# Query weights folded in three bursts instead of four, and the last tile of the hidden transform in slices of 384 and 128 columns

## The chip, the cores and the metric

One core of a Trainium2 chip. The metric is the device time of one launch, in microseconds; smaller is better. The core's engines run their own instruction streams: TensorE (PE; PEld is its weight load), VectorE (DVE), ScalarE (ACT), GpSimd (POOL) and SyncE (SP), which here only issues DMAs. PE accumulates into eight PSUM banks of 128 x 512 f32 (2 KB a partition). A float32 number is carried as a pair, high part and low part, and a product of two such matrices takes three matmuls.

## The reference

```python
def reference(A_x, A_dft_seq_re, A_dft_seq_im, A_dft_hid_re, A_dft_hid_im, B_x, B_w_q, B_k1, B_k2, B_u, B_v, gate_w):
    def _A_ref(x, dft_seq_re, dft_seq_im, dft_hid_re, dft_hid_im):
        a = jnp.einsum("bsd,ed->bse", x, dft_hid_re)
        b = jnp.einsum("bsd,ed->bse", x, dft_hid_im)
        y = jnp.einsum("ts,bse->bte", dft_seq_re, a) - jnp.einsum("ts,bse->bte", dft_seq_im, b)
        return y
    def _B_ref(x, w_q, k1, k2, u, v):
        q = jnp.einsum("nd,dhc->nhc", xf, w_q)
        s1 = jnp.einsum("nhd,ed->nhe", q[..., :dk], k1)
        s2 = jnp.einsum("nhd,ed->nhe", q[..., dk:], k2)
...
        act = _gelu(jnp.einsum("nd,nhkd->nhk", xf, ue))
        out = jnp.einsum("nhk,nhk,nhkd->nd", g, act, ve)
        return out.reshape(B, S, D)

    g = _sigmoid((x * gate_w).sum(-1, keepdims=True))
    a = _A_ref(x, A_dft_seq_re, A_dft_seq_im, A_dft_hid_re, A_dft_hid_im)
    b = _B_ref(x, B_w_q, B_k1, B_k2, B_u, B_v)
    return g * a + (1 - g) * b
```

Here x is 2048 x 640 (S x D), w_q is 640 x 32 x 256, k1 and k2 are 16 x 128, u and v 256 x 640. Branch A is a two-sided Fourier transform; branch B picks, for each token and head, the best two of 256 experts by the scores s1 and s2; g mixes the two.

## The kernel before

**Sequence transform.** The transform along the sequence runs first, in 128 *pieces*: two matrices (re, im), four chunks of 512 columns (TC) and, for each of them, 16 row tiles of x (NT). One piece multiplies five 128-column slices of an x tile (index d) with one 128 x 512 tile of the matrix: 5 x 3 = 15 matmuls, written by `mm3` (L140, L141, L142), accumulated in PSUM banks 0 to 4. After the 16th piece of a chunk ACT copies the five banks to the buffer ST (L248, called through `stage`), and the next piece, the first of the next chunk, opens the banks anew. DVE later multiplies ST by a row of gate values (L213, operand `grow`) and it goes to DRAM. A tile of the matrix is loaded (`wf`, L173) five pieces ahead, and split three pieces ahead: ACT takes its high part (L135), POOL or DVE subtracts it (L136). A tile of x is loaded as `xr`, split by `split_x` (ACT L135, DVE L136, into `X`), and summed against the gate's weights by `gate_sum` (DVE L314, into `zc`); behind piece 14 `gate` turns `zc` into g (ACT: table load and sigmoid, L541), and behind piece 15 `store_gate` writes it to DRAM in four small stores issued by ACT (L547, `gdr`). Split x tiles 0 to 11 are put away to DRAM one by one (`put_x`, L496, tile `xd`) so that their places are free, and come back later.

**Folding the query weights.** In the first 30 pieces (N0) the kernel also computes W' = w_q x keys, so that the scores need only x W' afterwards. W' has eight *groups* of four heads. A group has four w_q tiles of 640 KB (numbers 4G to 4G + 3, 32 tiles in all), and `w_part(m)` multiplies one of them: four matmuls of 32 x 320 (L405). Two tiles make a half group in bank 5, the next two in bank 6; behind each half DVE transposes it to SBUF (L411, `wp`), so a bank is free for the next group when that transpose is done. `split_w(G)` splits the group's result (ACT L135 and DVE L136, into `WU`); for groups 4 to 7 `make_t` and `split_t` also form sums of blocks. The tiles are multiplied in four *bursts* of two groups, behind pieces 10, 16, 22 and 27. A w_q tile is loaded on SP (L396) into a pool of five buffers, or into a place that is lent by something which is not in use just then: `LENT_WQ` names places of x tiles (X0 to X15) or of others, `LENT_U` two halves of the buffer `wqu`. The load waits until the last reader of that place is through.

**What sets the order.** `at(n, f)` hangs f behind piece n, and `follow(n)` calls what hangs there; each engine carries out its instructions in the order of these calls. So a load, a split or a sum that is hung one piece later stands later in the stream of SP, ACT or DVE, behind all that was hung before it. SP's and ACT's DMAs share eight slots, handed out in turn: an issue waits until the DMA that had the slot before has landed.

**The end.** After the pieces come the scores, the choice of experts, and 84 steps of the hidden transform. The last step's tile is 2 x 128 rows of d; its second half is held back and computed in two slices of columns of the same 512, each with 18 matmuls (six high and low pairs, three matmuls each), so that the first slice can be subtracted (DVE L1224) and stored (L1225, from SP, ACT, SP) while PE computes the second. The slices are 256 columns each (`c = TC // 2`).

Of the kernel before, what the change touches and what calls it, by code (L numbers as in the profile page):

```python
# [17 lines left out]
P = 128  # L18
S = 2048
D = 640  # L20
# [5 lines left out]
NT = S // P  # L26
NP = NT // 2
TC = 512
# [4 lines left out]
NG = HH // 8  # L33
# [73 lines left out]
def gated_mix_kernel(ctx: ExitStack, tc: tile.TileContext, xT, xn, dreT, dimT, wsre, wsim, wq, kT, uT, vv, gw, out):  # L107
# [14 lines left out]
    def bank(n, shape=(P, TC), dt=F32):  # L122
        return psum.tile(list(shape), dt, name=f"b{n}", tag=f"b{n}")
# [4 lines left out]
    ST = big.tile([P, 5, TC], F32, name="ST", tag="ST")  # L128
# [9 lines left out]
    def mm3(o, wh, wl, ah, al, first, last, more=False):  # L138

        nc.tensor.matmul(o, wh, ah, start=first, stop=False, skip_group_check=more)  # L140
        nc.tensor.matmul(o, wh, al, start=False, stop=False, skip_group_check=more)  # L141
        nc.tensor.matmul(o, wl, ah, start=False, stop=last, skip_group_check=more)  # L142
# [9 lines left out]
    def run_bg(us):  # L152
        bg.run(us, share)
# [38 lines left out]
    def at(n, f, *args):  # L192
        then.setdefault(n, []).append(lambda: f(*args))
# [57 lines left out]
    for q in range(2 * NC):  # L251
        n = NT * (q + 1)
# [84 lines left out]
    for n in range(WARM):  # L337
        c = slice(0, 2 * P) if n < WARM - 1 else slice(2 * P, TC)
# [41 lines left out]
    wqs, wps, wp = {}, {}, {}  # L380
    WQB = 5
    NWQ = 4 * NG
    BURST = 8
    LENT_WQ = {5: "X15", 6: "X14", 15: "xl", 16: "xf", 17: "xh", 23: "xl", 29: "X6", 30: "X7", 31: "X8"}
    LENT_U = {7: 1, 8: 0, 14: 1, 18: 0}

    def load_wq(m):


        if m in LENT_U:  # L390
            wqs[m] = wqu[:, LENT_U[m]]
        elif m in LENT_WQ:
            wqs[m] = big.tile([P, 4, HALF], F32, name="wq", tag=LENT_WQ[m])
        else:
            wqs[m] = p1.tile([P, 4, HALF], F32, name="wq", tag="wq", bufs=WQB)
        nc.sync.dma_start(wqs[m], wq[m // 4 * 4 + m % 2 * 2 + m // 2 % 2])  # L396
# [61 lines left out]
    xf, xs = {}, {}  # L458
# [40 lines left out]
        X[s] = place(tag)  # L499
        nc.sync.dma_start(X[s].bitcast(F32), xd[s])  # L500

    for s, b in enumerate((12, 14, 16, 17, 18, 19, 20, 21, 22)):
        at(b, put_x, s)
    for s, tag in ((11, "xh"), (12, "xl")):
        at(s + 12, move_x, s, tag)
    for n in range(NT - 4):
        at(n, load_x, n + 4)
    for n in range(NT - 3):
        at(n, split_x, n + 3)
    for n in range(NT - 2):  # L510
        at(n, gate_sum, n + 2)


    n = N0 - 1
    for B, b in enumerate((10, 16, 22, 27)):
        for m in range(BURST * B, BURST * (B + 1)):
            at(b, w_part, m)
        for G in (2 * B, 2 * B + 1):
            at(b, split_w, G)
            if G >= NG // 2:  # L520
                at(b + G % 2 * (G < NG - 1), make_t, G)
                at(b + 1 + G % 2 * (G < NG - 1), split_t, G)
    for b, m in enumerate((0, 1, 2, 3, 4, 5, 6, 7, 8)):
        at(b, load_wq, m)
    for m, b in enumerate((10, 10, 11, 11, 12, 13, 13, 15, 16, 16, 16, 17, 18, 19, 20, 20, 22, 22, 22, 22, 23, 24, 25), 9):
        at(b, load_wq, m)
    for s in range(9, AWAY):
        at(n - 3, put_x, s)
# [277 lines left out]
    for p in range(NP):  # L806
        n = N0 + 4 * p + min((p + 1) // 2, 3)
# [3 lines left out]
    for n in range(2 * NT + 3, 4 * NT + 3):  # L811
        s = n % NT
# [151 lines left out]
    def t_sum(k, n, a):  # L964

        m = 8 if k == KD else k
        if n < 2:
            return TS[m][:, (2 * n + a) * 2 * P:][:, :2 * P]
        if n == 2:
            return TS[5 + k // 2][:, (2 * (k % 2) + a) * 2 * P:][:, :2 * P]  # L970
        return right(0, a, k)[:, 2 * P:4 * P] if n == 3 else TS[m][:, PAIR + a * P:][:, :P]

    def right(w, a, k):
        return T[("xh", "xl")[a]][:, w] if k == KD else DD[k][:, w, a]
# [107 lines left out]
    for k, (n, m) in enumerate(((-1, 2), (0, 4), (5, 7), (7, 9), (10, 12))):  # L1082
        n, m = NT * (NC + 2) + n, NT * (NC + 2) + m
# [8 lines left out]
    def split_step(m):  # L1092
        if m < 2 * NSTEP:
            b, (u, k) = m // NSTEP, divmod(m % NSTEP, KZ)
            what = UNITS[u]
            key = (b, "s" if (b or k == KD) and what in ("s1", "s2", "s4") else what, k)
            sp[m] = ring(m)[:, 0], ring(m)[:, 1]
            split(raw[key], *sp[m], nc.vector if what in ("s2", "s3") else nc.gpsimd)
            bg.credit -= 0.8 if what in ("s2", "s3") else 0.0
            if what in ("a22", "s3", "s4") or k < KD and (b == 0 or what in ("a11", "a12")):  # L1100
                give(key)
# [30 lines left out]
    roles, res = {}, {"c22": ST[:, 0:2], "c": ST[:, 2:4]}  # L1132

    def put(b, row, d, f):
        c = slice((2 * b + row) * TC, (2 * b + row + 1) * TC)
        if d == 4:
            nc.scalar.dma_start(out[4][:, c], f)
        else:
            nc.scalar.dma_start(out[d:d + 2, :, c].rearrange("d p t -> p d t"), f)
# [33 lines left out]
    def step(m):  # L1173
        b, (u, k) = m // NSTEP, divmod(m % NSTEP, KZ)
        what = UNITS[u]
        if k == 0:
            if what in ("a11", "s1"):
                roles["W"] = bank(0)
            if what in ("a12", "a22"):
                roles["Z"] = [bank(2), bank(6)]  # L1180
            if what == "s1":
                roles["Y"] = [bank(3), bank(4)]
            if what == "a11":
                roles["X"] = [bank(5), bank(1)]
        split_step(m + AHEAD)
        o, w, w5 = {
            "a11": ("X", lambda a: right(0, a, k)[:, 0:2 * P], lambda a: right(0, a, k)[:, 4 * P:]),
            "a12": ("Z", lambda a: right(1, a, k)[:, 0:2 * P], lambda a: right(1, a, k)[:, 4 * P:]),
            "s1": ("Y", lambda a: t_sum(k, 0, a), lambda a: right(0, a, k)[:, 4 * P:]),
            "s2": ("X", lambda a: t_sum(k, 1, a), None),  # L1190
            "s4": ("Y", lambda a: right(1, a, k)[:, 2 * P:4 * P], None),
            "s3": ("X", lambda a: t_sum(k, 3, a), None),
            "a22": ("Z", lambda a: t_sum(k, 2, a), lambda a: t_sum(k, 4, a))}[what]
        h, l = sp.pop(m)
        more = what in ("s2", "s3", "s4")
        end = k == KD
        very_last = b == 1 and what == "a22"
        for d in range(1 if very_last else 2):
            c = slice(d * P, (d + 1) * P)
            mm3(roles[o][d], w(0)[:, c], w(1)[:, c], h, l, k == 0 and what in ("a11", "a12", "s1", "a22"), end, more)  # L1200
            run_bg(0.68)
        if very_last:
            held.append((t_sum(k, 2, 0)[:, P:], t_sum(k, 2, 1)[:, P:], h, l))
        if w5:
            mm3(roles["W"], w5(0), w5(1), h, l, k == 0 and what in ("a11", "s1"),
                end and what in ("a12", "a22"))
            run_bg(0.68)
        if not end:
            return
        if what in ("a12", "a22"):  # L1210
            f = ST[:, 4]
            nc.scalar.activation(f, roles["W"], AF.Copy)
            put(b, u // 6, 4, f)
        if what == "s3":
            at(NPC + m, post, b, what)
        elif not very_last:
            at(NPC + m + 1, post, b, what)
        else:
            z, c = (*roles["Z"], bank(7)), TC // 2
            for n, (d, r, eng) in enumerate(((0, slice(0, TC), nc.sync), (1, slice(0, c), nc.scalar), (1, slice(c, TC), nc.sync))):  # L1220
                if n:
                    for i, (wh, wl, h, l) in enumerate(held):
                        mm3(z[n][:, r], wh, wl, h[:, r], l[:, r], i == 0, i == KD)
                nc.vector.tensor_tensor(res["c"][:, d, r], res["c"][:, d, r], z[n][:, r], op=OP.subtract)  # L1224
                eng.dma_start(out[d][:, 3 * TC + r.start:3 * TC + r.stop], res["c"][:, d, r])  # L1225
# [61 lines left out]
    for m in range(2 * NSTEP):  # L1287
        share = 0.95 if m >= 5 else 0.0
        step(m)
        follow(NPC + m)  # L1290
        if m == NSTEP:
            bg.drain()
# [44 lines left out]
```

## Time and profile before

| | |
|---|---|
| median of 3 runs | 748.27 us (748.08 to 748.84) |
| the profiled execution, whole | 748.37 us |
| its span in the profile | 746.6 us |
| granted TensorE clock in the span | 1.0 |
| PE busy | 742.6 us |
| w_q loads into the pool and lent x places | 28 of 640 KB, 8.4 us from issue to landing |
| x tiles moved to DRAM | 11 of 640 KB, 9.7 us |
| sequence matrix tiles, first matrix | 63 of 256 KB, 6.8 us |

In the rows of the profile that follow, a row with a time is one instruction (start, duration, engine, line, operation, operands, shapes); what stands in brackets is how long its engine was idle before it and what ended that. A row without a time groups the instructions of a line: count, busy time and mean ns of one behind the bar, then the idle time ahead of them with its releaser. PE's instructions overlap, so their pace is read from their starts. `PEq`, `ACTq` and `SPq` rows are DMA issues.

### The profile page before, as it was taken

The page shows a single profiled execution, that of the slowest core. Times are in us where ns is not written, and L with a number is a line of the kernel's source. Part 1 is how long each engine was busy: PE and PEld are TensorE (multiplying, and loading weights), DVE is VectorE, ACT ScalarE, POOL GpSimd, SP SyncE. Part 2 cuts the span into 40 slices and gives each one's busy share as a digit, 9 for nine tenths or more (in the row PEclk, how much of TensorE's full clock was granted, in tenths as well). Part 3 has the DMA queues.
Part 4 walks back from the last instruction along what each step waited for, and adds up shares of the span by engine and source line. Part 5 has one row for each costly group of instructions (what it writes and reads, how often), then busy time and mean ns, then how long its engine had stood idle before and what let it go on. Part 6 is the DMA issues. An engine that isn't in the chain of part 4 may idle for free.

```text
span 746.6 us, 11142 instructions
## 1 busy us (share of the span) xinstructions
PE 742.6 (99%) x3923; PEld 604.7 (81%) x3923; DVE 579.7 (78%) x744; ACT 366.4 (49%) x664; POOL 343.4 (46%) x287
## 2 busy tenths in 40 slices
PE   9999999999999999999999999999999999999998
PEld 7877777888888888888888888888888888888887
DVE  7982277595999899999999888979799974367651
ACT  4434154553445745555453686633545643443351
POOL 5632424441532424245135456644455693487253
PEclk9999999999999999999999999999999999999999
DMA  9989999777656785971498676488856689775301
GB/s 336 403 310 373 413 375 380 217 226 221 155 158 151 192 246 136 254 201 63 124 403 279 151 172 193 138 258 283 286 200 197 228 265 334 224 234 175 113 29 71
DMA packets 84632, 171.11 MB, mean 229 GB/s; under 512 B 16096, under 2 KB 21600, under 8 KB 84320
## 3 DMA queue, kind: packets, MB, share of 16 engines
q1 hardware_dynamic: 71680, 147.44, 58.5%
q0 software_dynamic: 5472, 9.96, 8.5%
q10 hardware_dynamic: 7424, 13.00, 4.6%
q8 instruction: 31, 0.51, 0.3%
q14 instruction: 25, 0.20, 0.1%
HBM read 136.40 MB, written 32.39 MB: 226 GB/s over the span
## 4 chain that ended last, share of the span: by engine, by line
PE 99%; DVE 0%; issue 0%
PE b L140 31%; PE b L141 31%; PE b L142 31%; PE b L405 2%; PE b L240 2%; PE b L890 1%; PE b L339 0%; PE b L343 0%; DVE ST L1224 0%
## 5 line engine op out<-in xcount | busy, mean ns | idle before, releaser
L140 PE MATMUL b<-WS,X 128*128 128x512 f32 x620 | 242.9, 392 | 0.0
L141 PE MATMUL b<-WS,X 128*128 128x512 f32 x620 | 241.3, 389 | 0.0
L142 PE MATMUL b<-WS,X 128*128 128x512 f32 x620 | 241.3, 389 | 0.0
L136 POOL TENSOR_TENSOR WS<-wf,WS 128x512 fp32r<-128x512 f32 x89 | 133.5, 1502 | 163.9 <-ACT WS L135 157.0
L140 PEld LDWEIGHTS b<-WS,X 128*128 128x128 f32 x620 | 116.4, 188 | 26.3 <-issue 2.1
L142 PEld LDWEIGHTS b<-WS,X 128*128 128x128 f32 x620 | 116.4, 188 | 24.3
L141 PEld LDWEIGHTS b<-WS,X 128*128 128x128 f32 x620 | 116.4, 188 | 23.7
L135 ACT ACTIVATE WS<-wf 128x512 fp32r<-128x512 f32 x89 | 55.7, 627 | 82.8 <-PE b L142 51.9
L136 POOL TENSOR_TENSOR xl<-xf,xh 128x640 fp32r<-128x640 f32 x16 | 27.3, 1709 | 74.2 <-ACT xh L135 74.2
L878 DVE TENSOR_TENSOR hot<-rows,wtab 128x1024 f16<-128x1024 f16 x64 | 55.8, 897 | 5.6 <-PE b L890 5.6
L600 ACT ACTIVATE sc<-b 128x512 f32<-128x512 f32 x32 | 19.9, 621 | 78.8 <-PE b L142 75.0
L187 POOL DMA_DIRECT2D WS<-in_wsre x30 | 26.5, 882 | 61.8 <-ACT WS L185 60.5
L136 POOL TENSOR_TENSOR WS<-ra,WS 128x512 fp32r<-128x512 f32 x33 | 47.2, 1439 | 14.5 <-ACT WS L135 14.3
L848 ACT ACTIVATE b<-b,mask 128x128 f32<-128x128 f32 x128 | 43.1, 343 | 15.6 <-PE b L890 12.5
L135 ACT ACTIVATE WS<-ra 128x512 fp32r<-128x512 f32 x47 | 29.5, 631 | 43.0 <-PE b L142 25.7
L655 DVE TENSOR_TENSOR eq<-sc,mm 128x1024 f16<-128x1024 f32 x32 | 44.4, 1388 | 0.9
L662 DVE TENSOR_REDUCE tied<-eq 128x64 f32<-128x1024 f16 x32 | 39.0, 1219 | 0.9
L653 DVE TENSOR_REDUCE mm<-sc 128x64 f32<-128x1024 f32 x32 | 38.8, 1211 | 0.2
L213 DVE SCALAR_TENSOR_TENSOR ST<-ST,grow 128x512 f32<-128x512 f32 x40 | 29.7, 807 | 9.2 <-DMA grow<-gdr 9.2
L136 POOL TENSOR_TENSOR WP<-ra,WP 128x512 fp32r<-128x512 f32 x13 | 19.3, 1492 | 31.0 <-ACT WP L135 30.9
L140 PE MATMUL b<-WU,xh 128*128 128x512 f32 x80 | 31.2, 391 | 0.0
L142 PE MATMUL b<-WU,xl 128*128 128x512 f32 x80 | 31.1, 389 | 0.0
(218 smaller groups left out, 1447.4 us busy)
## 6 DMA issues: line engine op xcount, KB each, us to landing
X<-xd SPq DMA_DIRECT2D x36, 640.0 KB, 6.5
wq<-in_wq SPq DMA_DIRECT2D x28, 640.0 KB, 8.4
wf<-in_wsim SPq DMA_DIRECT2D x64, 256.0 KB, 4.7
wf<-in_wsre SPq DMA_DIRECT2D x63, 256.0 KB, 6.8
ra<-pd SPq DMA_DIRECT2D x40, 256.0 KB, 3.4
WS<-in_wsre POOLq DMA_DIRECT2D x30, 256.0 KB, 6.4
pd<-ST ACTq DMA_DIRECT2D x30, 256.0 KB, 4.8
xd<-X SPq DMA_DIRECT2D x11, 640.0 KB, 9.7
```

What stands on the lines that cost most here:

```text
L135: nc.scalar.activation(h, f, AF.Copy)
L136: eng.tensor_sub(l, f, h.bitcast(F32))
L140: nc.tensor.matmul(o, wh, ah, start=first, stop=False, skip_group_check=more)
L141: nc.tensor.matmul(o, wh, al, start=False, stop=False, skip_group_check=more)
L142: nc.tensor.matmul(o, wl, ah, start=False, stop=last, skip_group_check=more)
L187: nc.gpsimd.dma_start(l, (wsre, wsim)[w][c, s], accum_op=OP.add)
L213: nc.vector.scalar_tensor_tensor(f, f, -1.0 if w else 1.0, g, op0=OP.mult, op1=OP.mult)
L653: nc.vector.tensor_reduce(m, sc, op=OP.max, axis=AX.X)
L655: nc.vector.tensor_tensor(eq, sc, m[:, :, None].to_broadcast([P, HH, E]), op=OP.is_equal)
L662: nc.vector.tensor_reduce(tied[:, s, ib, :], eq, op=OP.add, axis=AX.X)
L848: nc.scalar.activation(f[:, :, n], f[:, :, n], AF.Copy, scale=mask4[:, n:n + 1])
L878: nc.vector.tensor_tensor(o, a, b, op=op)
```

## The change

The eight groups are folded in three bursts of 3, 3 and 2 groups, behind pieces 14, 21 and 27. The w_q tiles wait longer, so more of them need a lent place: tiles 8 and 9 lie in two halves of ST, tile 0 in the place of x tile 15, tiles 22 and 23 in those of x tiles 0 and 1. For this `split_x` and `gate_sum` of x tile 15 are called inside the first burst, behind group 0, while `split_w` of a burst's first group is called ahead of its third. The places of some `put_x` calls and of the w_q loads move with it. At the end, the two slices are 384 and 128 columns instead of 256 and 256.

```diff
-    BURST = 8
-    LENT_WQ = {5: "X15", 6: "X14", 15: "xl", 16: "xf", 17: "xh", 23: "xl", 29: "X6", 30: "X7", 31: "X8"}
-    LENT_U = {7: 1, 8: 0, 14: 1, 18: 0}
+    LENT_WQ = {0: "X15", 10: "xl", 11: "xf", 19: "xl", 20: "xf", 21: "xh", 22: "X0", 23: "X1", 29: "X6", 30: "X7", 31: "X8"}
+    LENT_U = {6: 1, 7: 0, 17: 1, 18: 0}
+    LENT_ST = {8: 0, 9: 1}
...
+        elif m in LENT_ST:
+            f = ST.rearrange("p a b -> p (a b)")[:, LENT_ST[m] * 2 * D:][:, :2 * D]
+            wqs[m] = f.rearrange("p (j c) -> p j c", j=4)
...
-    for s, b in enumerate((12, 14, 16, 17, 18, 19, 20, 21, 22)):
+    for s, b in enumerate((11, 12, 13, 16, 17, 18, 20, 21, 22)):
         at(b, put_x, s)
...
+    for n in range(NT - 4):
+        at(n, split_x, n + 3)
     for n in range(NT - 3):
-        at(n, split_x, n + 3)
-    for n in range(NT - 2):
         at(n, gate_sum, n + 2)
...
-    for B, b in enumerate((10, 16, 22, 27)):
-        for m in range(BURST * B, BURST * (B + 1)):
-            at(b, w_part, m)
-        for G in (2 * B, 2 * B + 1):
+    for b, G0, G1 in ((14, 0, 3), (21, 3, 6), (27, 6, 8)):
+        for G in range(G0, G1):
+            if G == G0 + 2:
+                at(b, split_w, G0)
+            for m in range(4 * G, 4 * G + 4):
+                at(b, w_part, m)
+            if G == 0:
+                at(b, split_x, NT - 1)
+                at(b, gate_sum, NT - 1)
+        for G in range(G0 + (G1 == G0 + 3), G1):
+            late = G == 5
             at(b, split_w, G)
             if G >= NG // 2:
-                at(b + G % 2 * (G < NG - 1), make_t, G)
-                at(b + 1 + G % 2 * (G < NG - 1), split_t, G)
-    for b, m in enumerate((0, 1, 2, 3, 4, 5, 6, 7, 8)):
-        at(b, load_wq, m)
-    for m, b in enumerate((10, 10, 11, 11, 12, 13, 13, 15, 16, 16, 16, 17, 18, 19, 20, 20, 22, 22, 22, 22, 23, 24, 25), 9):
+                at(b + late, make_t, G)
+                at(b + late + 1, split_t, G)
+    for m in range(10):
+        at(m, load_wq, m)
+    for m, b in enumerate((10, 12, 14, 14, 15, 15, 16, 16, 17, 17, 18, 18, 19, 20, 21, 21, 21, 22, 22, 23, 24, 25), 10):
         at(b, load_wq, m)
...
-            z, c = (*roles["Z"], bank(7)), TC // 2
+            z, c = (*roles["Z"], bank(7)), 3 * P
```

How it moves instructions is seen in the streams of three engines. In the rows that follow, `b_480` is a bank's tile, a `waits` list names the events that an issue waits for, and `xN` counts equal instructions in a row. The changed kernel's lines lie 3 to 10 further down (L411 is L414, L541 is L551, L547 is L557, L396 is L399, L496 is L499).

**DVE at the first burst.** First before (behind piece 10), from the last x tile ahead of it to the next one:

```order
L136 TENSOR_TENSOR X<-xr,X 128x640
L314 ISA xr,zc<-xr,gwb 128x640
L314 ISA zc 128x1
L411 STREAM_TRANSPOSE wp<-b_480 128x2x5x32
L411 STREAM_TRANSPOSE wp<-b_491 128x2x5x32
L411 STREAM_TRANSPOSE wp<-b_501 128x2x5x32
L411 STREAM_TRANSPOSE wp<-b_512 128x2x5x32
L136 TENSOR_TENSOR WU<-wp,WU 128x5x128 x2
L136 TENSOR_TENSOR X<-xr,X 128x640
```

and after (behind piece 14):

```order
L414 STREAM_TRANSPOSE wp<-b_569 128x2x5x32
L414 STREAM_TRANSPOSE wp<-b_580 128x2x5x32
L136 TENSOR_TENSOR X<-xr,X 128x640
L314 ISA xr,zc<-xr,gwb 128x640
L314 ISA zc 128x1
L414 STREAM_TRANSPOSE wp<-b_594 128x2x5x32
L414 STREAM_TRANSPOSE wp<-b_605 128x2x5x32
L136 TENSOR_TENSOR WU<-wp,WU 128x5x128
L414 STREAM_TRANSPOSE wp<-b_617 128x2x5x32
L414 STREAM_TRANSPOSE wp<-b_628 128x2x5x32
L136 TENSOR_TENSOR WU<-wp,WU 128x5x128 x2
```

The subtraction and the gate sum of x tile 15 now stand between the transposes of group 0 and those of group 1, and the subtraction of group 0's W' ahead of group 2's transposes.

**ACT between piece 12 and piece 16.** First before, up to the copies of the five banks and the gate's stores:

```order
L135 ACTIVATE X<-xr 128x640
L135 ACTIVATE WS<-wf 128x512 x2
L541 ACT_TABLE_LOAD
L541 ACTIVATE gt<-zc 128x16
L135 ACTIVATE WS<-wf 128x512
L248 ACTIVATE ST<-b_129 128x512
L248 ACTIVATE ST<-b_130 128x512
L248 ACTIVATE ST<-b_131 128x512
L248 ACTIVATE ST<-b_132 128x512
L248 ACTIVATE ST<-b_133 128x512
L547 DMA gdr<-gc 32x32 x4
```

and after:

```order
L135 ACTIVATE X<-xr 128x640
L135 ACTIVATE WU<-wp 128x5x128 x3
L551 ACT_TABLE_LOAD
L551 ACTIVATE gt<-zc 128x16
L135 ACTIVATE WS<-wf 128x512
L248 ACTIVATE ST<-b_129 128x512
L248 ACTIVATE ST<-b_130 128x512
L248 ACTIVATE ST<-b_131 128x512
L248 ACTIVATE ST<-b_132 128x512
L248 ACTIVATE ST<-b_133 128x512
L557 DMA gdr<-gc 32x32 x4
```

The three copies of W' of the first burst now stand just ahead of the gate's table load; before, its two copies stood behind piece 10, four pieces earlier.

**SP at the loads for the second burst**, with the events waited for. Before (the gate's stores have slots DMAHW4, 6, 0 and 1 in between):

```order
L396 DMA wq_731<-in_wq 128x1280 [waits DMAHW2_49,DVE_49]
L396 DMA wqu_87<-in_wq 128x1280 [waits DMAHW3_49,PE_49]
L396 DMA wq_734<-in_wq 128x1280 [waits DMAHW4_49,PE_49]
L173 DMA wf_736<-in_wsre 128x512 [waits DMAHW5_49,Pool_49]
L496 DMA xd_85<-X_193 128x1280 [waits DMAHW6_49]
L396 DMA wq_756<-in_wq 128x1280 [waits DMAHW7_49,PE_49]
```

and after (the gate's stores have slots DMAHW2, 4, 5 and 6 in between):

```order
L499 DMA xd_85<-X_193 128x1280 [waits DMAHW1_49]
L399 DMA wq_706<-in_wq 128x1280 [waits DMAHW2_49,PE_49]
L399 DMA wqu_87<-in_wq 128x1280 [waits DMAHW3_49,PE_49]
L173 DMA wf_709<-in_wsre 128x512 [waits DMAHW4_49,Pool_49]
L499 DMA xd_85<-X_219 128x1280 [waits DMAHW5_49]
L399 DMA wqu_87<-in_wq 128x1280 [waits DMAHW6_49,PE_49]
L399 DMA wq_730<-in_wq 128x1280 [waits DMAHW7_49,PE_49]
```

`wq_706` is w_q tile 16; in these rows it is the first issue behind the gate's stores in the ring, and `X_193`, x tile 3, the last ahead of them. Tile 16 and those that follow it belong to the second burst, behind piece 21.

## The prediction

> **What bounds the kernel now.** The page comes first: which engine is full, and what the chain of work that ended last is made of.
>
> ```profile
> span 746.6 us, 11142 instructions
> PE 742.6 (99%) x3923; PEld 604.7 (81%) x3923; DVE 579.7 (78%) x744; ACT 366.4 (49%) x664; POOL 343.4 (46%) x287
> PE 99%; DVE 0%; issue 0%
> ```
>
> PE is the bound from the first microsecond to the last and waits for nobody; what is left of the span is the last subtraction and store. The profiled execution took 748.37 us, 1.77 more than its span; the median of the runs is 748.27. A change can gain only by giving PE less to do or by shortening the tail behind it, and it loses every time PE has to wait. The number of matmul instructions stays the same but for nothing: only the places of the W' matmuls and the widths of the last 36 change. So the sum has five terms: a burst fewer, three places where PE may wait, and the tail.
>
> **A burst fewer.** Second view: PE in order of time at the second burst (start, duration).
>
> ```profile
> 67.12 0.39 PE L142 MATMUL b<-WS,X 128*128 128x512 f32 x1
> 67.44 0.74 PE L405 MATMUL b<-wqu,kp 128*32 128x320 f32 x8
> ...
> 71.24 0.72 PE L405 MATMUL b<-wq,kp 128*32 128x320 f32 x8
> 71.89 0.50 PE L140 MATMUL b<-WS,X 128*128 128x512 f32 x1
> 72.22 0.40 PE L141 MATMUL b<-WS,X 128*128 128x512 f32 x1
> ```
>
> The usual pace of a 512-column matmul is 0.227 us (two L142, 75 matmuls apart, in the next fence: 17.00/75). A half group (16 records of L405) takes 1.08 us, as the transposes that follow them show below (two lie between 44.80 and 46.96). From 67.12 to 72.22 there are two usual steps (0.45) and four half groups (4.31); 0.34 of the 5.10 is left, the price of going in and out. Three bursts pay it once less: **-0.34 us**.
>
> ```profile
> 721.66 0.39 PE L142 MATMUL b<-WS,vxl 128*128 128x512 f32 x1
> 738.66 0.39 PE L142 MATMUL b<-WS,ts 128*128 128x512 f32 x1
> ```
>
> **The first wait: the third group of the first burst.** Groups take PSUM banks 5 and 6 in turn, so the first half of group 2 may start only when DVE has transposed the first half of group 1. With two groups nothing else stood between the transposes. Now x tile 15, whose place the first w_q tile borrows, is split and summed on DVE between the second and the third.
>
> ```profile
> 42.44 0.83 DVE L136 TENSOR_TENSOR X<-xr,X 128x640 fp32r<-128x640 f32 x1 [0.41 <-ACT X L135]
> 43.18 0.82 DVE L314 CUSTOM_DVE_ANT_0 xr<-xr,gwb 128x640 f32<-128x640 f32 x1
> 43.93 0.51 DVE L411 STREAM_TRANSPOSE wp<-b 128x320 f32<-128x320 f32 x1
> 44.80 0.52 DVE L411 STREAM_TRANSPOSE wp<-b 128x320 f32<-128x320 f32 x1 [0.37 <-PE b L405]
> ...
> 46.96 0.52 DVE L411 STREAM_TRANSPOSE wp<-b 128x320 f32<-128x320 f32 x1 [0.56 <-PE b L405]
> 47.40 0.78 DVE L136 TENSOR_TENSOR WU<-wp,WU 128x640 fp32r<-128x640 f32 x1
> 68.80 0.52 DVE L411 STREAM_TRANSPOSE wp<-b 128x320 f32<-128x320 f32 x1 [8.78 <-PE b L405]
> L314 DVE CUSTOM_DVE_ANT_0 xr<-xr,gwb x16: 811/1906/1918, 10.0 to 54.2; 128x640 f32<-128x640 f32 x16
> ```
>
> Count from the burst's first matmul. The first transpose starts at 1.36 (68.80 less 67.44), the second at 2.44. An operation behind a transpose starts 0.44 later (46.96 to 47.40), so the subtraction of x tile 15 at 2.88, the gate sum 0.74 behind it (3.62), the third transpose 0.75 behind that (4.37); it ends at 4.88, and PE goes on at about 4.97. PE itself is there at 4 x 1.08 = 4.31: **+0.66 us**. Bounds: 0 if DVE could start both operations ahead of the transposes (its order forbids it), and 1.7 if the gate sum takes 1.91, its median, as it does with POOL at work beside it. POOL's last subtraction before the burst belongs to piece 17 and is due at the start of piece 14, over 3 us earlier, and the next one comes a piece later: I take the 0.82.
>
> **The second wait: piece 16.** Piece 16 opens banks 0 to 4 anew and needs ACT to have copied piece 15's banks to ST. ACT used to have nothing else there; now three copies of W', the table load and the sigmoid stand just ahead, the last W' copy behind the burst's last transpose.
>
> ```profile
> 47.51 0.74 ACT L135 ACTIVATE WU<-wp 128x640 fp32r<-128x640 f32 x1 [1.42 <-DVE wp L411]
> 48.16 0.62 ACT L135 ACTIVATE WS<-wf 128x512 fp32r<-128x512 f32 x1
> 48.67 0.72 ACT L135 ACTIVATE X<-xr 128x640 fp32r<-128x640 f32 x1
> 58.05 1.28 ACT L541 ACT_TABLE_LOAD   x1
> 59.34 0.22 ACT L541 ACTIVATE gt<-zc 128x16 f32<-128x16 f32 x1
> 61.43 3.32 ACT L248 ACTIVATE ST<-b 128x512 f32<-128x512 f32 x5
> 64.21 2.15 ACTq L547 DMA_DIRECT2D gdr<-gc  x4
> 739.08 0.60 ACT L1212 ACTIVATE ST<-b 128x512 f32<-128x512 f32 x1 [5.75 <-PE b L142]
> ```
>
> Count from E, the first matmul of piece 15. The last transpose starts at 0.14 later than E (by the same spacing, 72.03 against 71.89) and ends at 0.66; the W' copy starts 0.03 behind (47.48 to 47.51), at 0.69; table load at 1.34 (47.51 to 48.16), sigmoid at 2.63 (58.05 to 59.34), the copy of piece 18's tile at 2.85, the first ST copy 0.51 later (48.16 to 48.67) at 3.36, done at 3.96, PE released at about 4.0. PE gets there at 0.33 + 14 x 0.227 = 3.51, and starting again from an empty array costs the 0.1 that 71.89 to 72.22 shows over the usual pace: **+0.6 us**. Bounds 0.4 and 0.75, for a copy 0.1 to either side. The other four banks are copied at 3.32/5 = 0.66 each, faster than the 0.68 after which PE asks for the next.
>
> **The third wait: the last w_q tile of the second burst.** SP issues loads in order, eight in flight, and the four small stores of the gate (L547, from ACT) take slots of the same ring. They stand behind the ST copies, and SP's load of w_q tile 16 now stands behind the first of them.
>
> ```profile
> 68.25 0.33 SPq L396 DMA_DIRECT2D wqu<-in_wq  x1
> 69.18 0.33 SPq L396 DMA_DIRECT2D wq<-in_wq  x1
> DMA to landing us min/median/max: 4.7/4.9/5.4
> DMA to landing us min/median/max: 1.8/2.1/2.4
> DMA to landing us min/median/max: 3.9/3.9/3.9
> DMA packets 2036, 7.03 MB, mean 414 GB/s; under 512 B 226, under 2 KB 334, under 8 KB 2035
> ```
>
> The three landing rows are those of the gate stores (L547), of the last stores of the output (L1225), and of the w_q load that SP issued at 43.18 after a pause; the last row is all DMA from 76 to 93 us. Before, SP held a w_q load until 69.18, 0.1 behind the first gate store's landing (64.21 + 4.9): the slot is a real wait. There the ring was full; now SP's last transfer (x tile 3) lands near E + 5.6, so the gate stores, issued from E + 5.5, meet an empty ring, as the last output stores do: 2.1 us. SP goes on at E + 7.6, tile 16 lands 3.9 later at E + 11.5. Up to tile 23 there follow seven w_q tiles and three x tiles of 640 KB, four sequence tiles and one gate row of 256 KB: 7.86 MB at 414 GB/s, 19.0 us, so E + 30.5. PE wants tile 23 at 4.1 (piece 16) + 6 x 3.40 + 0.1 + 11 x 0.54 = E + 30.5. It is a tie: **+0.15 us**, with bounds 0 and 3.0 (the gate stores at 4.9).
>
> ```profile
> L213 DVE SCALAR_TENSOR_TENSOR ST<-ST,grow 128x512 f32<-128x512 f32 x40 | 29.7, 807 | 9.2 <-DMA grow<-gdr 9.2
> ```
>
> DVE's part of that burst is free: the gate row lands near E + 20, and its five products, 0.81 us each, end before the first transpose at E + 25.9. The third burst keeps its two groups and its place. The sequence tiles of pieces 20 to 23 land before E + 21, more than a piece ahead of their splits.
>
> **The tail.** The last tile's second half is 36 matmuls, 18 for each slice.
>
> ```profile
> 738.88 0.28 PE L140 MATMUL b<-WP,ts 128*128 128x256 f32 x1
> 741.04 0.28 PE L140 MATMUL b<-WP,ts 128*128 128x256 f32 x1
> 743.08 0.28 PE L142 MATMUL b<-WS,ts 128*128 128x256 f32 x1
> 738.40 0.69 DVE L1224 TENSOR_TENSOR ST<-ST,b 128x512 f32<-128x512 f32 x1 [6.16 <-PE b L142]
> 743.39 0.42 DVE L1224 TENSOR_TENSOR ST<-ST,b 128x256 f32<-128x256 f32 x1 [1.73 <-PE b L142]
> L140 PEld LDWEIGHTS b<-WS,X 128*128 128x128 f32 x620 | 116.4, 188 | 26.3 <-issue 2.1
> L405 PEld LDWEIGHTS b<-wq,kp 128*32 128x32 f32 x224 | 6.9, 109 | 8.1 <-issue 1.1 <-DVE wp L411 0.8
> ```
>
> At 256 columns the pace is 2.16/18 = 0.120, at 512 it is 0.227: 0.107 for 256 columns and 0.013 fixed. 384 columns lie between, 0.173, so the first slice takes 3.12 (+0.96). For 128 columns the same line gives 0.067, 1.20 in all (-0.96): nothing won or lost on PE. But every matmul needs 128 columns of weights loaded first, and a load of 128 columns takes 188 ns, one of 32 columns 109: 0.82 ns a column, 105 ns for 128 columns. Only while the matmul streams longer than that is the load hidden. At 128 columns it is not: I take 0.105 + 0.013 = 0.118, bounds 0.067 and the 0.120 of 256 columns. The second slice takes 2.12, PE ends +0.92; the last matmul is 0.05 shorter, the last subtraction 0.13 (0.27 per 256 columns), the last store, 64 KB less, at most 0.16: **+0.6 us**.
>
> [...]
>
> **Sum.** -0.34 + 0.66 + 0.6 + 0.15 + 0.6 = +1.67. The span of 746.6 becomes 748.3, the profiled execution 750.0; on the median, 748.27 + 1.67 = **749.9 us**.
>
> **The rivals.** (1) *Not slower: the weight loads keep up.* If 128 columns load in 0.067 us or less, the tail is -0.33, the sum +0.7, 749.0. For it: no row has f32 matmuls of 128 columns one behind the other. Against: the two rows of weight loads above. (2) *The third wait decides.* If the gate stores land as late as before (4.9), everything behind them in the ring is 2.8 us later and PE stands for 3.0: 752.8; half of it gives 751.3. For it: no other row of L547. Against: the ring is empty. (3) *No wait at all*: if DVE and ACT get through in time, only -0.34 and the tail are left: 748.5. Against: their orders are fixed. (4) (1) and (3) together: 747.6, the only way below the old time, and still within 0.2%.
>
> **How the numbers follow.** 0.2%, 1.5 us, is about what a measurement of this kernel tells from no change. The forecast, 749.4 to 750.5, has 0.52: 0.32 of it beyond 749.8, 0.20 short of it. Rival 1 has 0.13 (same), rival 2 0.24 (slower), rival 3 0.09 (same), rival 4 0.02. Faster 0.02, same 0.42, slower 0.56. The range leaves out about 0.1 on each side: 748.6 to 751.7.
>
> **What would show it.** In the changed profile: three runs of L408 of 6.5, 6.5 and 4.3 us; in the first a gap of 0.66 before the ninth w_q tile, released by DVE's transpose; 0.5 before piece 16, released by ACT L248; the landing of w_q tile 23 against its use; and the pace of the last 18 matmuls, 0.118 or 0.067. A pace of 0.067, or a second burst without or with a long gap, makes the prediction wrong.

## The result, and the profile after

The changed kernel takes 754.09 us (median of 6 runs, 751.88 to 755.86), the kernel before 748.75 (6 runs, 748.08 to 749.28): a ratio of 1.0072, with an interval of 1.0054 to 1.0090. The direction was forecast; the size was not: +5.3 us instead of +1.7, and 754.1 lies above the range (748.6 to 751.7). The profiled execution took 753.50, 1.8 more than its span. Of the kernels below, one execution of pool_gate (3292.09 us) and the profiled one of three_clean (1068.11 us, granted clock 0.655) fell in a slow state, and the ratios leave them out.

The page's first lines and its chain of work:

```profile
span 751.7 us, 11149 instructions
PE 744.7 (99%) x3923; PEld 606.2 (81%) x3923; DVE 584.0 (78%) x744; ACT 366.1 (49%) x664; POOL 343.3 (46%) x287
PE 95%; DMA 3%; SPq 0%; DVE 0%; ACT 0%; issue 0%; ACTq 0%
```

PE was 99% of the chain before, with no DMA in it; now 3% are transfers. The view of what PE waited for (total us, times, longest) names the places:

```profile
PE b L408 <- DMA wq<-in_wq: 2.5, 1, 2.5
...
PE b L408 <- DVE wp L414: 0.5, 1, 0.5
PE b L140 <- ACT ST L248: 0.3, 1, 0.3
```

All three waits of the prediction are there, each released as it said, but the one that was to be the smallest is by far the largest. Now the same places in PE's timeline, first the first burst and piece 16:

```profile
55.23 0.39 PE L142 MATMUL b<-WS,X 128*128 128x512 f32 x1
55.54 3.44 PE L408 MATMUL b<-wq,kp 128*32 128x320 f32 x48
...
60.55 1.28 PE L408 MATMUL b<-ST,kp 128*32 128x320 f32 x16 [0.49 <-DVE wp L414]
...
62.84 0.50 PE L140 MATMUL b<-WS,X 128*128 128x512 f32 x1
63.17 0.39 PE L141 MATMUL b<-WS,X 128*128 128x512 f32 x1
...
66.15 0.39 PE L142 MATMUL b<-WS,X 128*128 128x512 f32 x1
66.85 0.50 PE L140 MATMUL b<-WS,X 128*128 128x512 f32 x1 [0.32 <-ACT ST L248]
67.19 0.40 PE L141 MATMUL b<-WS,X 128*128 128x512 f32 x1
```

Idle times in brackets count from the modelled end of a matmul, so the starts are the better measure. From 55.23 to 63.17 there are 7.94 us; six half groups (6.47), two usual steps (0.45) and one entry and exit (0.34) make 7.26: the first wait costs 0.68. From 66.15 to 67.19 there are 1.04 for two steps: the second costs 0.59. Then the second burst's last w_q tile, and the matmuls behind it:

```profile
92.39 1.26 PE L408 MATMUL b<-wq,kp 128*32 128x320 f32 x16
96.18 0.86 PE L408 MATMUL b<-wq,kp 128*32 128x320 f32 x8 [2.53 <-DMA wq<-in_wq]
96.96 0.80 PE L140 MATMUL b<-WS,X 128*128 128x512 f32 x1
97.56 0.63 PE L141 MATMUL b<-WS,X 128*128 128x512 f32 x1
...
99.69 0.58 PE L140 MATMUL b<-WS,X 128*128 128x512 f32 x1
100.11 0.39 PE L141 MATMUL b<-WS,X 128*128 128x512 f32 x1
```

Two things happen. PE stands 2.7 us longer than a step between two tiles takes (its own spacing there is 2.96, against 0.25). And behind the stop its matmuls come 0.43 apart instead of 0.227. The view by stretches (length, PE busy and instructions, granted clock, DMA share, GB/s) says why:

```profile
93.27:96.68 3.41, 0.88 (x16) 1.00 1.02 408
96.68:100.10 3.42, 3.42 (x11) 0.50 1.02 422
```

The granted clock is 0.50 for 3.41 us. At the pace of a burst before, the matmul at 100.11 would have come 2.34 us behind the one at 96.18 (0.65 to the first L140, 0.33, six steps of 0.227); it came 3.93 behind it. The slow clock costs 1.6 us, a term that the prediction did not have.

### The profile page after: what moved, and what is told of

The parts are those of the page before. It is cut to its first block, busy times and chain, and to the rows that moved or that the text cites. A ratio compares the mean times of both kernels' runs of the same rounds, so it can differ in the third digit from the quotient of the medians.

```text
span 751.7 us, 11149 instructions
## 1 busy us (share of the span) xinstructions
PE 744.7 (99%) x3923; PEld 606.2 (81%) x3923; DVE 584.0 (78%) x744; ACT 366.1 (49%) x664; POOL 343.3 (46%) x287
## 4 chain that ended last, share of the span: by engine, by line
PE 95%; DMA 3%; SPq 0%; DVE 0%; ACT 0%; issue 0%; ACTq 0%
PE b L140 30%; PE b L142 30%; PE b L141 30%; PE b L240 2%; DMA wq<-in_wq 2%; DMA grow<-gdr 1%; PE b L408 1%; PE b L900 1%; PE b L339 0%; SPq L399 0%; ACT L551 0%; DVE wp L414 0%; SPq L173 0%; PE b L343 0%; DVE xr L314 0%
## 5 line engine op out<-in xcount | busy, mean ns | idle before, releaser
L140 PE MATMUL b<-WS,X 128*128 128x512 f32 x620 | 243.6, 393 | 0.3 <-ACT ST L248 0.3
L140 PEld LDWEIGHTS b<-WS,X 128*128 128x128 f32 x620 | 116.7, 188 | 26.6 <-issue 1.7
L213 DVE SCALAR_TENSOR_TENSOR ST<-ST,grow 128x512 f32<-128x512 f32 x40 | 31.5, 847 | 18.2 <-ACT WS L135 18.2
L140 PE MATMUL b<-WU,xh 128*128 128x512 f32 x80 | 31.1, 389 | 0.0
L141 PE MATMUL b<-WU,xh 128*128 128x512 f32 x80 | 31.1, 389 | 0.0
```

Source lines behind the costliest of these rows:

```text
L213: nc.vector.scalar_tensor_tensor(f, f, -1.0 if w else 1.0, g, op0=OP.mult, op1=OP.mult)
```

## The experiments

**Is it SP's pause behind the gate's stores?** In the changed kernel SP and ACT issue at these times:

```profile
63.50 0.33 SPq L499 DMA_DIRECT2D xd<-X  x1
66.63 0.34 ACTq L557 DMA_DIRECT2D gdr<-gc  x1
70.51 0.33 SPq L399 DMA_DIRECT2D wq<-in_wq  x1
DMA to landing us min/median/max: 2.9/3.4/3.8
```

(The last row is that of the four stores; the first took the 3.8.) SP stands from 63.8 to 70.5, until the first store has landed, 0.06 earlier. If the stores take none of the slots, this pause cannot be. One word of the changed kernel is edited:

```diff
-            nc.scalar.dma_start(gdr.rearrange("(i j p) -> j i p", j=4, p=32)[j], gc[32 * j:32 * j + 32])
+            nc.gpsimd.dma_start(gdr.rearrange("(i j p) -> j i p", j=4, p=32)[j], gc[32 * j:32 * j + 32])
```

> The changed kernel with the four gate stores issued by GpSimd's queue instead of ScalarE's, so that they take none of the eight slots that SP's loads use. Theory: SP's loads no longer stop behind the stores, w_q tile 23 lands some 5 us earlier, PE's stop of 2.5 us in the second burst goes and with it the 3.4 us at half clock (1.4 us): -4.0 us on the changed kernel, 750.0. Rival 1, the DMA rate alone is too low for the ten MB between the bursts: tile 23 is still 1 us or more late, about 752. Rival 2, GpSimd's issues (4 of some 0.9 us) and their wait for the gate hold up its splits of sequence tiles: a new stop of PE before pieces 18 to 20, 751 or more.

Measured: 749.98 (ratio to before, 748.95 on this chip, 1.0015, interval 1.0006 to 1.0024). That is 4.1 us less than the changed kernel (4.3 when each is compared with the kernel before of its own session); the theory said 4.0. PE's waits are now

```profile
PE b L339 <- PEq L1339: 0.8, 1, 0.8
PE b L408 <- DVE wp L414: 0.5, 1, 0.5
PE b L140 <- ACT ST L248: 0.3, 1, 0.3
```

(the first row is the start of the program, as before the change). The w_q wait is gone, and the granted clock stays at 1.00 (from 62 to 94, mean 0.999). By the trace's landings tile 23 was there at 93.55, and its use came at 94.4: 0.9 us of room. The stores took 4.8 to 5.3 us on GpSimd's queue, where ACT's took 2.9 to 3.8 in the changed kernel, and the w_q tiles were in time all the same. Both rivals fall.

**The DMA rate behind the pause.** DMA in the changed kernel, by stretches of 4 us (the columns are granted clock, DMA share and GB/s):

```profile
70.00:74.00 4.00, 1.00 0.61 197
74.00:78.00 4.00, 1.00 0.90 272
78.00:82.00 4.00, 1.00 1.00 416
```

and in pool_gate, without the pause:

```profile
70.00:74.00 4.00, 1.00 1.01 411
74.00:78.00 4.00, 1.00 1.02 422
```

Tile 16 was issued at 70.51 and landed at 74.36, and even then the rate is not the 414 GB/s that I took: 272 GB/s for 4 us more, with eight transfers queued. By the landings, tile 17 came 3.33 us behind tile 16, where 640 KB take 1.57 in the stream that runs (89.71 to 91.28). pool_gate has a slow stretch too, 342 and 326 GB/s from 62 to 70, behind the place where the changed kernel's transfers pause at 57 (55 GB/s from 56 to 58); it makes no tile too late. The kernel before shows the same some 8 us behind its own pause at 43, in a stretch that the prediction does not use:

```profile
52.00:54.00 2.00, 1.00 0.93 250
```

To see whether the first profile was an accident, the changed kernel ran once more.

> The changed kernel once more, for a second profile. Theory: SP again stops behind the four gate stores, one of the transfers behind the pause again takes about 3 us instead of 1.6, w_q tile 23 lands 1 to 4 us after PE asks for it, and where the stop is long the clock is halved behind it. Rival: the slow transfers of the first profile were an accident of that execution: tile 23 is less than 0.5 us late and the run is near 750.5.

Measured: 755.00 in the profiled run, 752.59 in the other (mean clock 0.998 and 1.0). SP stood again until the first store had landed (71.64), tile 17 came 3.47 us behind tile 16, the x tile ahead of tile 23 came 2.74 behind its forerunner, PE's spacing at tile 23 was 3.48, and the clock was halved for 3.41 us behind it. The theory holds. A slow stretch behind a pause is what the kernel before (250 GB/s) and both profiles of the changed one (272 GB/s in the first, 3.47 us for one tile in the second) have in common. That the pause makes it slow was not tried by itself. The kernel before also has such a stretch without a pause (305 GB/s from 68 to 72, with 411 in the 4 us ahead of it), so something else can do it too.

**What halves the clock?** The kernel before, with reductions on DVE (results unused) that hold up the transposes, so that PE stands in all four bursts:

```diff
+    STOPS = (3, 5, 7, 9)
+    idle = const.tile([P, 10], F32, name="idle")
...
         if r == 1:
+            for i in range(STOPS[G // 2] if G % 2 == 0 and n == 0 else 0):
+                nc.vector.tensor_reduce(idle[:, i:i + 1], ps[:, :HALF], op=OP.max, axis=AX.X)
```

> The kernel before, with 3, 5, 7 and 9 reductions of 128x320 on VectorE (results unused) ahead of the first transpose of its four bursts, so that PE stands still for about 1.1, 2.0, 2.9 and 3.8 us in them. Theory: the granted clock is halved for some 3.4 us behind stops from about 2.5 us on (the changed kernel's stop of 2.5 us was followed by 3.4 us at 0.50) and stays at 1 behind shorter ones: here behind the third and the fourth, about 9.8 us of stops and 2 x 1.4 us of slow clock, 761. Rival: the drop came from something else near it (the mixture of tiles, the transfers): no row below 0.9 behind any stop, 758.5.

> As stops_up with 9, 7, 5 and 3 reductions. Theory: the drop goes with the length of the stop, not with its place: half clock behind the first and the second burst only, 761. Rival: it goes with the place (the second burst, or the later ones).

Measured: 758.30 and 759.87 (stops_up), 759.15 and 760.65 (stops_down). The stops, by PE's idle time, were 0.8, 1.6, 2.4 and 3.2 us in the one, 3.6, 2.4, 1.6 and 0.8 in the other. Theory and rivals failed alike: in stops_up the clock fell behind the third stop, but not behind the longer fourth; in stops_down behind the first only. What sorts them is a grid. In the traces of the kernel before and of the changed one, the time from the clock's first rise to every later change is a whole number of 3.413 us (217 times that before; 27, 28 and 219 in the changed kernel); the first rise itself lies 5.44 us into the span in the one and 4.52 in the other. In stops_up and stops_down a halved stretch fills 3.42 us as well. So PE's busy time is read in windows of this length, counted from the clock's changes. stops_up:

```profile
97.04:100.45 3.41, 1.02 (x19) 1.00 0.78 278
100.45:103.87 3.42, 3.42 (x28) 0.50 0.68 226
120.93:124.35 3.42, 2.31 (x33) 1.00 0.97 273
124.35:127.76 3.41, 1.34 (x20) 1.00 0.84 342
127.76:131.17 3.41, 3.41 (x27) 1.00 0.74 230
```

stops_down:

```profile
45.09:48.50 3.41, 0.33 (x8) 1.00 0.98 383
48.50:51.92 3.42, 3.42 (x32) 0.50 1.05 372
75.81:79.22 3.41, 1.65 (x26) 1.00 0.82 194
79.22:82.63 3.41, 3.41 (x24) 1.00 0.97 386
```

In these rows the windows with 1.34 us or more of PE work are followed by full clock, those with 1.02 or less by half; in the changed kernel a window with 0.88 is followed by half. The stop of 3.2 us lay across an edge and left 2.31 and 1.34; the one of 2.4 lay within one window. In after_again the window ahead of the 3.41 us at 0.50 had 1.27. So the windows ahead of a fall were idle for 2.1 to 3.1 us of their 3.4. From this follow two estimates for these kernels: a stop is safe below about 2 us (3.41 less 1.34), and between that and some 4 us (twice as much, for a stop that an edge halves) chance decides, if the windows begin at another place in each execution, as the first rises at 5.44 and 4.52 suggest. It would explain a part of the scatter of the changed kernel: its run at 751.88 has a mean clock of 1.0, those from 753.45 to 755.08 have 0.998, and the one at 755.86 has 0.995; one window of 3.41 us at half clock makes 0.0023 of 752 us, two make 0.0045.

**The other two waits.** As pool_gate, with x tile 15's subtraction behind group 1 and its sum behind group 2, and the gate two pieces later:

```diff
-            if G == 0:
+            if G == 1:
                 at(b, split_x, NT - 1)
-                at(b, gate_sum, NT - 1)
+        if G0 == 0:
+            at(b, gate_sum, NT - 1)
...
-    at(NT - 2, gate)
-    at(NT - 1, store_gate)
+    at(NT, gate)
+    at(NT + 1, store_gate)
```

(and for the first chunk `load_row` and `gate_piece` four pieces later).

> As pool_gate, and x tile 15 is split behind the transposes of group 1 and summed behind those of group 2, and the gate's sigmoid, stores, row load and products are hung two to four pieces later. Theory: the stop of 0.5 us ahead of the third group and that of 0.5 us ahead of piece 16 both go: 1.0 us less than pool_gate, 749.0. Rival: the work only stands elsewhere in front of what PE needs (piece 15's x tile, the second burst's transposes) and less than 0.4 us is won.

Measured: 748.87 (ratio 0.9999, 0.9991 to 1.0008), 1.1 us less than pool_gate. PE's timeline at the first burst:

```profile
55.80 0.39 PE L142 MATMUL b<-WS,X 128*128 128x512 f32 x1
56.12 3.44 PE L408 MATMUL b<-wq,kp 128*32 128x320 f32 x48
...
62.72 0.50 PE L140 MATMUL b<-WS,X 128*128 128x512 f32 x1
63.06 0.40 PE L141 MATMUL b<-WS,X 128*128 128x512 f32 x1
...
66.70 0.39 PE L142 MATMUL b<-WS,X 128*128 128x512 f32 x1
66.93 0.39 PE L140 MATMUL b<-WS,X 128*128 128x512 f32 x1
```

From 55.80 to 63.06 there are 7.26, no wait, and entry and exit cost 0.34 also in a burst of three groups. Piece 16's matmuls follow 0.23 apart. Both waits are gone, and nothing took their place.

**The tail alone.** The kernel before with one edit:

```diff
-            z, c = (*roles["Z"], bank(7)), TC // 2
+            z, c = (*roles["Z"], bank(7)), 3 * P
```

> The kernel before with slices of 384 and 128 columns, nothing else. Theory: at 128 columns the weight load (about 0.111 us) sets the pace, not the stream; PE ends 0.8 us later, the last subtraction and store win back 0.3: +0.5 us on before (749.2). Rival: the pace is proportional to columns, nothing is lost on PE and the smaller last store wins 0.3: -0.3 us (748.4).

Measured: 749.48 against 748.95 (ratio 1.0006, 0.9997 to 1.0015): the +0.5 of the theory, but the interval does not part it from no change. The timeline does, here that of the changed kernel, which has the same tail:

```profile
743.57 0.33 PE L140 MATMUL b<-WP,ts 128*128 128x384 f32 x1
...
746.71 0.22 PE L140 MATMUL b<-WP,ts 128*128 128x128 f32 x1
746.77 0.27 PE L141 MATMUL b<-WP,ts 128*128 128x128 f32 x1
...
748.56 0.27 PE L142 MATMUL b<-WS,ts 128*128 128x128 f32 x1
```

Behind the first, the matmuls of 128 columns come 1.79/16 = 0.112 apart; in proportion to the columns it would be 0.067. Their weight loads start 0.112 apart as well (746.82 to 748.50, 15 steps). From the first to the last of the 36 starts it takes 4.99 us, 0.79 more than before (738.88 to 743.08).

**What is left of three bursts.** pool_late_gate with slices of 256 columns again (`TC // 2`):

> As pool_late_gate, with the last tile of d in two slices of 256 columns as before. Theory: all that is left of the change is one burst's entry and exit less, -0.34 us on before: 748.4, and 0.5 us less than pool_late_gate. Rival: something else in the three bursts costs as much, and it is no faster than before (748.75 or more).

Measured: 748.87, ratio 0.9998 (0.9989 to 1.0007): inconclusive, since 0.34 us is half of what the interval leaves open to either side. Its other runs scatter from 748.06 to 749.65. In pool_late_gate tile 23 had landed only 0.4 us ahead of its use, so it got more room:

```diff
-    for s, b in enumerate((11, 12, 13, 16, 17, 18, 20, 21, 22)):
+    for s, b in enumerate((11, 12, 13, 16, 17, 18, 21, 21, 22)):
         at(b, put_x, s)
```

> As three_clean, with put_x of x tile 6 hung behind piece 21 instead of 20, so that SP issues w_q tile 23 ahead of that transfer. In the profile of pool_late_gate tile 23 landed only 0.5 us before its use. Theory: in part of three_clean's executions (748.06 to 749.65) tile 23 was still up to 1 us late; with 1.5 us more room the upper part goes and the median is 748.3. Rival: the scatter has another cause, which the kernel before shares (748.40 to 749.94): the median stays near 748.8.

Measured: 748.43 against 748.73, ratio 1.0000 (0.9991 to 1.0009), 748.03 to 750.45. The median is the theory's, the interval is not; tile 23 now landed at 90.29, 2 us sooner than in pool_late_gate (92.27), and still some runs are long: the scatter hardly comes from that tile, and the kernel before has it too. No version beats the kernel before by what can be measured.

**The stores in ACT's queue, but later.** If their place among SP's loads decides, ACT may keep them. The changed kernel with

```diff
-    at(NT - 1, store_gate)
+    at(NT + 6, store_gate)
```

(`load_row` and `gate_piece` of the first chunk six pieces later)

> The changed kernel with the gate stores still issued by ScalarE in the same eight slots, but hung behind piece 22 instead of 15 (the gate row and its products six pieces later as well), so that in the ring they stand behind the loads of the second burst. Theory: what counts is where the stores stand among SP's loads, not which engine issues them: no pause of SP before tile 16, no stop in the second burst, 750.0 as with GpSimd's queue. Rival 1, the queue they share is what costs: about 754 as the changed kernel. Rival 2, the pause moves to the loads of the third burst and stops PE there: 751 to 753, with the stop at the last w_q tiles.

Measured: 752.20 (ratio 1.0044, 1.0027 to 1.0060). PE's longest wait:

```profile
PE b L408 <- DVE wp L414: 3.4, 2, 2.9
```

The two windows of the clock's grid around it:

```profile
115.95:119.36 3.41, 2.07 (x32) 1.00 1.03 410
119.36:122.78 3.42, 1.87 (x28) 1.00 0.83 339
```

The w_q wait of the second burst is gone with the same queue. But the five products of the gate row (3.95 us on DVE) now stand ahead of the third burst's transposes and stop PE for 2.9 us: my edit's own wait, of neither theory. (It fell across an edge, and the clock stayed.) So the products went behind the third burst, two pieces later still:

> As act_late, with the five products of the gate row hung behind piece 28, that is behind the third burst. In act_late the second burst had no stop, but these products, hung behind piece 26, stood on VectorE ahead of the third burst's transposes and stopped PE for 2.9 us there. Theory: without that stop what is left is the changed kernel without its third wait, 749.5 to 750.0, the same as with GpSimd's queue: the place of the stores among SP's loads decides, not the engine that issues them. Rival: the pause of SP behind the stores now makes w_q tiles 28 to 31 late and PE stops for a w_q tile in the third burst: 751 or more.

Measured: 760.02 (1.0162, 1.0144 to 1.0181).

```profile
PE b L140 <- ACT ST L248: 7.7, 2, 7.4
```

Again no PE wait for a w_q tile, and again a new one: SP's stores of the multiplied ST have to follow the late products, PE waits 7.4 us for ACT's copy to ST (no matmul from 136 to 142), and the clock is halved for 6.8 us, two windows (0.50 from 140 to 145, 0.54 and 0.55 in the microseconds to either side). Both kernels missed their forecast time. For the question asked they agree with the theory, and no more than that.

## Why the prediction was wrong

| term | predicted | measured |
|---|---|---|
| a burst fewer | -0.34 | -0.34 by the spacing in pool_late_gate |
| first wait, DVE between transposes | +0.66 | +0.68 |
| second wait, ACT ahead of piece 16 | +0.6 | +0.59 |
| third wait, w_q tile 23 | +0.15, at most 3.0 | +2.7 (3.2 in the second profile) |
| tail | +0.6 | +0.45 to the end of the span |
| clock behind the third wait | none | +1.6 |

The terms measured make 5.7, while 5.1 lies between the two profiled executions (753.50 and 748.37). The changed one had reached its 101st matmul 0.4 us earlier (23.27, before 23.70), which is most of the difference.

**A burst fewer, the first two waits and the tail** stand with their mechanisms (the -0.34 by the spacing of the matmuls alone, since no kernel's time resolves it). In the tail PE lost 0.79 instead of 0.92, since the pace at 128 columns is 0.112 and not 0.118; the last subtraction and store won what was forecast.

**The third wait failed, in one step of its sum.** Its times count from E, the first matmul of piece 15, at 62.84. SP was to go on at E + 7.6 and did at E + 7.7, by luck, since errors cancelled. ACT issued the first store at E + 3.8, between its copies and not behind them. And the ring was not empty: x tile 3, which was to land near E + 5.6, landed at 70.29 (E + 7.45), and the store 0.16 behind it, 3.8 us after its issue and not 2.1. Tile 16 was to land at E + 11.5, and did. PE was to want tile 23 at E + 30.5 and wanted it at E + 30.6. But "7.86 MB at 414 GB/s, 19.0 us" took 21.8: the rate was read from a stretch in which the stream had long been running, and used for one that begins with a pause. Where PE and the transfers were to tie, they were 2.7 us apart.

By the landings, 1.8 us of the excess lies between tiles 16 and 17 (3.33 instead of 1.57), in the stretch at 272 GB/s; why the rate is low there stays open. The other 1.1 came at the end: the x tile ahead of tile 23 landed 2.71 behind its forerunner, at a full rate in the windows. One transfer more stands beside it in the DMA view of 91.5 to 95 (packets, MB, share of 16 engines):

```profile
q8 instruction: 1, 0.02, 2.0%
```

It is a fetch of instructions, one packet, and 2.0% of 16 engines for 3.5 us is 1.1 us on one of them. If the x tile's part on that engine came 1.1 us later for it, so did the landing of the tile. But the kernel before has one at 86.79 too (1.7% of 16 engines from 86 to 90), and there the next tile of 640 KB lands 1.54 behind its forerunner. So this cause is possible and not shown.

**The clock was put at nothing.** The sum has no term for what a stop of PE does to its clock, and gives no reason; it cost 1.6 us, all of it behind the third wait.

**The rival that decided** had this place and nearly this price (3.0), but another cause, stores that land late; SP went on when it was to, so that the price fits is chance. And its 752.8 lacked the clock: with the 1.6 us behind the stop it would have been 754.4, near the 754.09 for the wrong reason. A range that took the rival's bound and the clock together would have held the result.

## What to carry to other kernels

A load whose arrival ties with its use is not worth a few tenths: behind it stands the whole of the slower case, here 2.7 us of waiting and 1.6 of slow clock. Take the rate of a transfer stream from the stretch that looks like the one in question, and one that restarts from a row behind an earlier pause. When small stores share slots with another engine's loads, ask what is in the ring when they are issued; and when work is moved to cure a wait, look at what it then stands in front of on every engine that handles its result.

## What the runs showed of the hardware

- The granted clock changed at whole numbers of 3.413 us behind its first rise (217 before; 27, 28 and 219 in the changed kernel), and the first rise came 5.44 and 4.52 us into the span. Windows of this length with 0.33, 0.88, 1.02 and 1.27 us of PE work were followed by 3.41 us at 0.50, those with 1.34, 1.65, 1.87 and 2.31 by full clock. In stops_up half clock followed a stop of 2.4 us and not one of 3.2, so the length of the stop alone does not tell.
- Behind a pause of the transfers a 640 KB transfer came 3.33 us behind its forerunner in the changed kernel, 3.47 in its second profile and 3.32 in the kernel before (52.79 to 56.11), instead of 1.57, though more were queued. A stretch at 305 GB/s without a pause, in the kernel before, leaves the cause open.
- ACT's DMA issues ran while its copies ran: the first gate store was issued at 66.63, ahead of four of the five copies that precede it in the program.
- An f32 matmul of 512 columns behind new weights took 0.227 us, one of 384 columns 0.174 (3.14/18), one of 256 0.120, one of 128 0.112: from 256 to 128 columns 0.008 is won.
